# Weight rounding in the first segment of a RetNet and SwiGLU kernel: VectorE's steps regrouped, tiles loaded and rounded later

## The chip, the cores and the metric

One core of one Trainium2 chip runs the kernel. The metric is the device time of one execution in microseconds (us). The kernel before takes 743.69 us, the median of three runs (743.6 to 743.85).

Engines in the profile: PE is TensorE's matmuls, PEld its weight loads, DVE is VectorE, ACT is ScalarE, POOL is GpSimd, SP is SyncE, which issues the loads. "L446" is line 446 of the kernel that was profiled, so one statement has another number in each kernel; each fence says which kernel it shows.

## The reference, cut to what matters

```python
def _attn_ref(q, k, v):               # 4 batches, 8 heads, 768 steps, head size 64
    for t in range(S):
        state = gamma * state + outer(k[t], v[t])
        y[t] = scale * q[t] @ state
def _moe_ref(x, w_gate, w_val, w_out):     # 3072 tokens, 512 -> 1536 -> 512
    g = x @ w_gate
    return (g * sigmoid(g) * (x @ w_val)) @ w_out
```

The three weight matrices reach the kernel as 64-bit floats and have to be rounded to 32-bit ones on the chip.

## The kernel before

The tokens are worked through in segments. Only the first segment matters here. It has three parts: the **retention** of its six chunks (some 40 us), twelve **up blocks** (some 9.5 us each; block f multiplies with up tile f), and the down products. A weight tile that arrives as 64-bit words is rounded in three stages on three engines. The buffer in which it arrives is its raw place, which the next load takes when the last stage is done:

```python
    def convert_a(piece, *own):                  # ScalarE
        if piece in raw:
            d, lo, hi = words_of(piece)
            nc.scalar.activation(d, hi.bitcast(F32), AF.Abs)
            signs[piece] = []
            for i, o in enumerate(own):          # the sign words go to PSUM banks
                nc.scalar.copy(banks[o], hi[:, ts(i, 512)].bitcast(F32))
                signs[piece].append(banks[o])
            nc.scalar.activation(lo.bitcast(F32), lo, AF.Copy, scale=2.0 ** -51, bias=2.0)

    def convert_b(piece):                        # VectorE
        if piece in raw:
            d, lo, hi = words_of(piece)
            nc.vector.tensor_scalar(d, d, ..., op0=ALU.min, op1=ALU.max)           # SBUF only
            u = d.bitcast(U32)
            nc.vector.tensor_scalar(u, u, 3, None, op0=ALU.logical_shift_left)     # SBUF only
            for i, t in enumerate(signs.pop(piece)):
                v = u[:, ts(i, 512)]
                nc.vector.scalar_tensor_tensor(v, t.bitcast(U32), 0x80000000, v,   # reads a bank
                                               op0=ALU.bitwise_and, op1=ALU.bitwise_xor)

    def convert_c(piece):                        # GpSimd, then the next load into the raw place
        if piece in raw:
            d, lo, hi = words_of(piece)
            nc.gpsimd.tensor_tensor(d.bitcast(I32), d.bitcast(I32), lo.bitcast(I32), op=ALU.add)
            del raw[piece]
        load_next(piece[0])
```

An up block works with a scheme of seven products (as Strassen's), each of four TensorE instructions. Wherever products are counted below, one such instruction is meant, so a block has 28. `s1` to `s4` are sums of the block's input, made by VectorE in the retention; the sixteen instructions with T1, T2, B22 and T3 are the products on sums. `sums_t` makes the tile's sums T1, T2 and T4, three subtractions within SBUF. The order of the calls is the order of the instructions on each engine:

```python
    def up(f):
        ...
        product(x, B11, a_up(0, 0));  nc.scalar.copy(p1, x)       # x: bank f % 2
        if f:
            left[f - 1][0]()                       # gates of the block before (product T4, ScalarE)
        if f + 1 < NF:
            sums_t(("up", f + 1, 0))
        product(wb, T1, s1);  nc.scalar.copy(p5, wb)
        for p in at_block[f]:                      # one "down" half tile and up tile f + 2
            convert_b(p)
        for p in at_block[f][::-1]:
            convert_c(p)
        product(x, T2, s2, start=False);  nc.scalar.copy(u2, x)   # accumulates on x, after the copy p1
        product(wb, B22, s4, start=False)
        if f:
            left.pop(f - 1)[1]()                   # gate multiplications of the block before
        tt(hT[:, f, 0], wb, u2, op=add)
        product(x, T3, s3, start=False)
        tt(hT[:, f, 1], x, p5, op=add)
        for i, p in enumerate(at_block[f + 1] if f + 1 < NF else []):
            convert_a(p, *((6, 7) if p[0] == "up" else ((4, 6)[i],)))
        product(z, B21, a_up(0, 1))
        tt(c11, z, p1, op=add)
        left[f] = gates, muls
```

The retention is a list of steps, and the rounding of the first tiles is set between them:

```python
    for n in range(2, len(cs)):
        load_chunk(cs[n], early[4 * n : 4 * n + 4])
        if n in (2, 4):
            load_next("up")
    ...
    retain(7);  convert_a(u0, 0, 1)
    retain(3);  convert_b(u0);  convert_c(u0)
    retain(3);  sums_t(u0)
    retain(3);  convert_a(u1, 2, 3)
    retain(2);  convert_b(u1);  convert_c(u1)
    retain(len(steps))
    convert_a(("down", 0, 0), 4);  convert_a(u2, 6, 7)
```

## Time and profile before

| | before |
|---|---|
| median of three runs | 743.69 us |
| profiled run (742.34 us, not one of the three): span, mean TensorE clock | 740.6 us, 0.998 |
| TensorE busy | 96% of the span |
| one up block (from block 7's to block 8's first product on sums) | 119.69 − 110.03 = 9.66 us |
| 28 products of a block at full rate (the prediction's estimate) | 9.03 us |

On the profile's page, a group of instructions is read like this: line, engine, operation, output and inputs with shapes and count, then busy time and mean ns of one, then the idle time of the engine just ahead of them and who ended most of it. The up products before:

```profile
L435 PE MATMUL bank<-xs,ring 128*128 128x384 f32 x192 | 65.7, 497 | 2.8 <-DVE xs L418 2.8
L435 PE MATMUL bank<-xT,ring 128*128 128x384 f32 x144 | 51.0, 492 | 3.7 <-DVE hT L453 3.7
```

The 3.7 us are the small waits for L453, the last gate multiplication of the block before, one in nearly every block; the 2.8 us are one wait at the end of the retention. There is no long gap anywhere in the up blocks.

### The profile page before, as it was taken

The numbers are of one execution on the slowest core, as the hardware profiler recorded it, in microseconds if no ns is written. First come the engines' busy times: TensorE is split into PE (matmuls) and PEld (weight loads), VectorE is DVE, ScalarE is ACT, GpSimd is POOL, SyncE is SP. The second block draws the span as 40 slices with busy tenths as digits, with TensorE's granted clock in tenths as the row PEclk, the third lists the DMA queues.
The fourth block names the chain that finished last, engine by engine and source line by source line (L and its number), as shares of the span: only waits on it lengthen the run. The fifth ranks groups of instructions, "written<-read, shape, count | busy, mean of one in ns | idle before, by whom it ended". The sixth has DMA issues, their size and how long they took to land.

```text
span 740.6 us, 11633 instructions
## 1 busy us (share of the span) xinstructions
PE 712.9 (96%) x4516; PEld 614.0 (83%) x4516; DVE 482.6 (65%) x829; ACT 241.8 (33%) x484; POOL 244.5 (33%) x152
## 2 busy tenths in 40 slices
PE   5789999999999999999999999999999999999997
PEld 5645555568888999997888999998888899999886
DVE  2899999997595787877454465758426356667420
ACT  2587777421211333321211324332121133233000
POOL 2533333423100547381210173454310053726000
PEclk9999999999999999999999999999999999999999
DMA  9968886458968667670643355660283055540010
GB/s 328 375 214 255 254 265 214 150 205 272 317 220 332 235 228 260 247 270 28 192 180 127 105 209 204 208 205 22 85 308 131 30 200 199 199 150 1 0 58 29
DMA packets 60823, 139.04 MB, mean 188 GB/s; under 512 B 4576, under 2 KB 27616, under 8 KB 60768
## 3 DMA queue, kind: packets, MB, share of 16 engines
q1 hardware_dynamic: 57312, 132.01, 52.2%
q10 hardware_dynamic: 3456, 6.29, 2.4%
q8 instruction: 35, 0.57, 0.3%
q14 instruction: 20, 0.16, 0.1%
HBM read 101.72 MB, written 36.57 MB: 187 GB/s over the span
## 4 chain that ended last, share of the span: by engine, by line
PE 82%; DVE 7%; issue 4%; POOL 2%; DMA 2%; ACT 2%; ACTq 0%; SPq 0%; DVEq 0%; POOLq 0%
PE bank L548 38%; PE bank L632 25%; PE bank L435 6%; PE bank L641 4%; PE bank L328 3%; PE bank L380 3%; PE bank L376 2%; POOL ring L265 2%; DVE ring L277 2%; PE bank L359 1%; DMA hT<-in_q_t_dram 1%; DMA hT<-in_k_t_dram 1%; DMA tab<-in_decays_dram 1%; DVE ring L252 1%; DVE xs L418 0%
## 5 line engine op out<-in xcount | busy, mean ns | idle before, releaser
L548 PE MATMUL bank<-loadp,ring 128*128 128x192 f32 x720 | 140.5, 327 | 2.8 <-ACT midp L513 2.8
L632 PE MATMUL bank<-wot,hsp 128*128 128x256 f32 x576 | 131.5, 383 | 0.0
L548 PEld LDWEIGHTS bank<-loadp,ring 128*128 128x128 f32 x720 | 120.5, 190 | 4.2 <-ACT midp L513 4.0
L632 PEld LDWEIGHTS bank<-wot,hsp 128*128 128x128 f32 x576 | 107.6, 190 | 16.3 <-issue 0.5
L513 DVE TENSOR_TENSOR iop<-bank,iop 128x384 f32<-128x384 f32 x144 | 79.7, 555 | 56.7 <-PE bank L548 53.6
L548 PE MATMUL bank<-xs,ring 128*128 128x192 f32 x432 | 87.8, 326 | 0.0
L513 POOL TENSOR_TENSOR iop<-hsp,midp 128x768 f32<-128x768 f32 x9 | 16.3, 1816 | 189.6 <-ACT hsp L513 149.4
L583 POOL TENSOR_TENSOR hT<-iop 128x768 f32<-128x768 f32 x36 | 66.5, 1848 | 35.8 <-DVE iop L513 35.8
L513 ACT COPY hsp<-bank 128x384 f32<-128x384 f32 x90 | 42.9, 479 | 99.5 <-PE bank L548 88.8
L548 PEld LDWEIGHTS bank<-xs,ring 128*128 128x128 f32 x432 | 73.1, 190 | 0.0
L435 PE MATMUL bank<-xs,ring 128*128 128x384 f32 x192 | 65.7, 497 | 2.8 <-DVE xs L418 2.8
L548 PE MATMUL bank<-xT,ring 128*128 128x192 f32 x324 | 66.2, 327 | 1.1 <-DVE iop L513 1.1
L632 PE MATMUL bank<-wot,hT 128*128 128x256 f32 x288 | 66.3, 383 | 0.0
L435 PEld LDWEIGHTS bank<-xs,ring 128*128 128x128 f32 x192 | 37.2, 194 | 29.5 <-DVE xs L418 3.4
L632 PEld LDWEIGHTS bank<-wot,hT 128*128 128x128 f32 x288 | 53.7, 190 | 8.5 <-issue 1.4
L548 PE MATMUL bank<-hsp,ring 128*128 128x192 f32 x288 | 56.8, 327 | 0.0
L513 DVE TENSOR_TENSOR midp<-bank,midp 128x384 f32<-128x384 f32 x72 | 40.0, 555 | 25.8 <-PE bank L548 24.3
L548 PEld LDWEIGHTS bank<-xT,ring 128*128 128x128 f32 x324 | 54.8, 190 | 2.3 <-DVE iop L513 2.2
L435 PE MATMUL bank<-xT,ring 128*128 128x384 f32 x144 | 51.0, 492 | 3.7 <-DVE hT L453 3.7
L548 PEld LDWEIGHTS bank<-hsp,ring 128*128 128x128 f32 x288 | 48.3, 190 | 0.5 <-ACT hsp L513 0.5
L435 PEld LDWEIGHTS bank<-xT,ring 128*128 128x128 f32 x144 | 26.5, 190 | 25.4 <-issue 9.0
L383 ACT COPY xT<-bank 128x512 f32<-128x512 f32 x24 | 14.1, 587 | 99.4 <-PE bank L380 96.6
(138 smaller groups left out, 983.4 us busy)
## 6 DMA issues: line engine op xcount, KB each, us to landing
ring<-unitt SPq DMA_DIRECT2D x50, 896.0 KB, 4.6
unitt<-ring SPq DMA_DIRECT2D x21, 896.0 KB, 4.6
unitb<-ring SPq DMA_DIRECT2D x12, 896.0 KB, 5.9
ring<-unitb SPq DMA_DIRECT2D x21, 512.0 KB, 5.7
out_dram<-iop ACTq DMA_DIRECT2D x24, 256.0 KB, 4.0
loadp<-in_w_val_dram SPq DMA_DIRECT2D x18, 256.0 KB, 5.8
loadp<-in_w_gate_dram SPq DMA_DIRECT2D x9, 512.0 KB, 6.4
midp<-in_w_out_dram SPq DMA_DIRECT2D x12, 256.0 KB, 3.1
```

The lines of the kernel that those rows point to most:

```text
L265: nc.gpsimd.tensor_tensor(d.bitcast(I32), d.bitcast(I32), lo.bitcast(I32), op=ALU.add)
L277: sub(both, w[:, ds(B22, 2)], w[:, ds(B12, 2)], op=ALU.subtract)
L328: nc.tensor.matmul(sp[i][:, ts(n, P)], kt[r, n], qt[r, n], start=True, stop=True, skip_group_check=True)
L376: nc.tensor.matmul(y[r, ts(n, P)], prev[r, n], qd[r, n], start=(n == 0), stop=False, skip_group_check=True)
L380: nc.tensor.matmul(y[ds(D * i, D), ts(n, P)], vn[:, ts(2 * n + i, D)], a[i][:, n], start=(ci == 0 and n == 0), stop=True, skip_group_check ...
L383: nc.scalar.copy(xT[:, :, c // NCK % 2, ts(ci % L, P)], pairs(y))
L435: nc.tensor.matmul(o, w[:, slot, k], a[:, k], start=(start and k == 0), stop=(stop and k == KH - 1), skip_group_check=True)
L513: events.append((t, len(events), lambda: fn(*args, **kw)))
L548: nc.tensor.matmul(o[:, h], w[:, h, slot], rhs, start=(start and h == 0), stop=True, skip_group_check=True)
L583: by_block(9.5, 13.5, lambda r: pool(to[:, r], u2[:, r], p5[:, r], op=add))
L632: nc.tensor.matmul(o, a[:, k], wot[k][:, slot], start=(start and k == 0), stop=(k == FH - 1), skip_group_check=True)
L641: nc.tensor.matmul(o, a_dn(0, 0, u)[:, k], wot[k][:, B11], start=(k == 0), stop=(k == FH - 1), skip_group_check=True)
```

## The change

What it does: VectorE's SBUF-only steps of both tiles of a block come first and its steps with a bank operand after them, and GpSimd adds the small tile first, so that GpSimd's additions fall beside VectorE instructions with a bank operand. The retention holds less rounding: the first two up tiles are loaded one chunk later, tile 0 is rounded in parts and later, tile 1 after the last sums, tile 2 inside block 0. The down tiles move back by one block up to block 5. ScalarE's table is loaded at the start.

```diff
-    def convert_a(piece, *own):
+    def convert_a(piece, own, part=None):          # the three ScalarE stages can be called apart
...
-    def convert_b(piece):
+    def convert_b(*pieces):
+        for p in pieces:                           # SBUF only: clamp and shift of every piece
...
+        for p in pieces:                           # then the steps with a bank operand
...
-    at_block = [[("down", n // 2, n % 2) for n in range(2 * FH) if f == min(n, NF - 2)] +
-                [("up", f + 2, 0)] * (f + 2 < NF) for f in range(NF)]
+    halves = [("down", n // 2, n % 2) for n in range(2 * FH)]
+    late_piece = {0: ("up", 2, 0), 5: halves[5]}
+    at_block = [[]] + [halves[f - (f < 6) : f + (f > 5) + (f == NF - 2)] +
+                       [("up", f + 2, 0)] * (f + 2 < NF) for f in range(1, NF)]
...
-        if f + 1 < NF:
+        if 1 < f < NF - 1:
             sums_t(("up", f + 1, 0))
+        if f == 0:
+            convert_a(late_piece[f], (6, 7), 0)
         product(wb, T1, s1)
+        convert_b(*at_block[f])
         for p in at_block[f]:
-            convert_b(p)
-        for p in at_block[f][::-1]:
             convert_c(p)
...                                                # parts 1 and 2 of tile 2 follow in block 0
+        elif f in late_piece:
+            convert_a(late_piece[f], (4,))
...
+        if f < 2:
+            sums_t(("up", f + 1, 0))
+        if f in late_piece:
+            convert_b(late_piece[f])
+            convert_c(late_piece[f])
...
+    nc.scalar.activation(warm, warm, AF.Silu)      # table load at the start
...
-        if n in (2, 4):
+        if n in (3, 5):
             load_next("up")
-    for _ in range(4):
+    for _ in range(3):
         load_next("down")
...
-    retain(7);  convert_a(u0, 0, 1)                # (calls joined in one line here)
-    retain(3);  convert_b(u0);  convert_c(u0)
-    retain(3);  sums_t(u0)
-    retain(3);  convert_a(u1, 2, 3)
-    retain(2);  convert_b(u1);  convert_c(u1)
-    retain(len(steps))
-    convert_a(("down", 0, 0), 4);  convert_a(u2, 6, 7)
+    retain(10);  convert_a(u0, (0, 1), 0);  retain(1);  convert_a(u0, (0, 1), 1)
+    retain(1);   convert_a(u0, (0, 1), 2);  retain(2);  convert_b(u0)
+    retain(2);   convert_c(u0)
+    retain(1);   convert_a(u1, (1, 3), 0);  retain(1);  convert_a(u1, (1, 3), 1)
+    sums_t(u0)
+    retain(len(steps))
+    convert_a(u1, (1, 3), 2);  convert_b(u1);  convert_c(u1)
```

## The prediction

> **What bounds the kernel now.** I read the busy shares first: TensorE is busy for 96% of the span. Then I read the stretches of ten microseconds, because the change touches only the first segment. That is the retention (0 to 42 us) and twelve "up" blocks of the weight tiles (42 to 162 us). From 140 us on TensorE is at 10.00 of 10 in nearly every stretch, and no line after that is changed. Columns: PE, PEld, DVE, ACT, POOL busy us (x instructions), TensorE clock, DMA share, GB/s.
>
> ```profile
> 20.00:30.00 10.00, 7.14 (x126) 6.06 (x120) 8.79 (x11) 6.53 (x15) 7.62 (x5) 1.00 1.07 374
> 30.00:40.00 10.00, 7.14 (x100) 5.43 (x100) 9.83 (x16) 4.92 (x15) 4.15 (x4) 1.00 0.84 291
> 40.00:50.00 10.00, 8.63 (x22) 4.94 (x23) 9.10 (x17) 7.98 (x13) 2.49 (x2) 0.83 0.75 234
> 90.00:100.00 10.00, 9.62 (x30) 5.43 (x29) 9.32 (x16) 7.38 (x13) 3.99 (x3) 1.00 0.82 253
> ```
>
> In the retention VectorE is full (9.83) and TensorE waits. In the blocks TensorE has 9.62 of 10 and VectorE 9.3. The timeline shows why: one block, then the end of the retention.
>
> ```profile
> 87.22 2.41 POOL L265 TENSOR_TENSOR ring<-ring,loadp 128x1024 int32<-128x1024 int32 x1 [6.00 <-ACT ring L241]
> 88.08 2.82 PE L435 MATMUL bank<-xT,ring 128*128 128x384 f32 x8 [0.40 <-DVE hT L453]
> 89.59 1.28 POOL L265 TENSOR_TENSOR wot<-wot,midp 128x512 int32<-128x512 int32 x1
> 89.66 1.75 DVE L277 TENSOR_TENSOR ring<-ring 128x512 f32<-128x512 f32 x1 [0.34 <-POOL ring L265]
> 91.45 0.42 DVE L278 TENSOR_TENSOR ring<-ring 128x256 f32<-128x256 f32 x1
> ```
>
> ```profile
> 38.64 2.39 POOL L265 TENSOR_TENSOR ring<-ring,loadp 128x1024 int32<-128x1024 int32 x1 [5.85 <-ACT state L353]
> 38.75 2.56 DVE L418 TENSOR_TENSOR xs<-xT 128x256 f32<-128x256 f32 x1
> 41.35 0.43 DVE L419 TENSOR_TENSOR xs<-xs,xT 128x256 f32<-128x256 f32 x1
> 41.37 7.12 PE L435 MATMUL bank<-xs,ring 128*128 128x384 f32 x16 [2.75 <-DVE xs L418]
> ```
>
> L277 takes 1.75 us beside a GpSimd addition and 0.68 us at 42.49, where GpSimd is idle. L418 takes 2.56 beside L265 and 0.43 alone. Both end about half a microsecond or less after GpSimd does: they wait, they are not slowed. In each block the next tile's first product then waits 0.3 to 0.5 us for L453, the last VectorE gate multiplication. The first sixteen products on xs take 7.12 us; sixteen elsewhere take 5.32. The finer windows give the reason:
>
> ```profile
> 42.00:43.00 1.00, 1.00 (x3) 0.62 (x2) 1.00 (x3) 1.00 (x2) 0.00 (x0) 0.50 0.69 201
> ```
>
> The clock was half from about 41.3 to 44.9, after a gap of 2.75 us.
>
> **What the Trainium skill says.** "SBUF — State Buffer", section "Who interferes with whom": VectorE and GpSimd share one port pair under an exclusive lock. A VectorE instruction with two SBUF inputs, or in a two-port mode, blocks against GpSimd for the whole instruction; with at most one SBUF input outside those modes it doesn't. The trace agrees: L258 (one bank operand) stays at 0.65 us beside GpSimd, L252 goes from 0.69 to 1.04, L255 from 0.69 to 1.65. "TensorE: Matmul & The Clock Gate", Part 1: an idle window of about 3.4 us, free-running, halves the clock until a busy one. Here 2.75 us was enough, and the half clock lasted about 3.6 us. "ScalarE: Activation LUTs", section "What ACT_TABLE_LOAD costs": 1283 ns a load; the trace has 1.28 us, at 0.73 and again at 51.76.
>
> **The change part by part.** I took the new order of every engine and laid the measured durations along it (an estimate by hand).
>
> *Blocks, a gain.* GpSimd now adds the small "down" tile before the "up" tile, and VectorE's four SBUF-only steps precede its three bank steps. So GpSimd's 1.29 + 2.41 us fall beside the bank steps, the gate multiplications and the evictions, all with a bank operand. L277 should fall to 0.68 (1.07 us less) and VectorE from 9.3 to 8.2 us a block. TensorE is then the limit: 28 products at 5.16/16 = 0.3225 us (90.73 to 95.89) make 9.0 us. The last tiles agree: from 136.69 to 145.80, where nothing waits, is 9.1. Before, the eight blocks from 59.06 to 136.69 took 77.6 us; at 9.1 they take 72.8. Worth 4.8 us.
>
> *Loading order.* The first tile (1 MB, 2.8 us at 375 GB/s) now comes after chunk 3, the second after chunk 5. From the bytes moved, chunk 3's queries land at about 15.7 instead of 18.35. Chunk 4 has the same megabytes before it as ever, and lands at about 21.6. So the early arrival is mostly lost again: the fourth scores start at 21.6, and eviction (L383 before, 0.6) and decay (L353, 1.07) put the state addition of chunk 3 at about 26.6.
>
> *Retention, VectorE.* Rounding of tile 0 moves behind that addition: 0.4 + 0.69 + 0.70 + 1.3 us. Then the sums of the second pair 1.75 and the last mask. Uncontended this ends at about 31.4. GpSimd's last scalings (some 1.6 us of blocking) and its addition for tile 0 (2.4 us, which gets the port after the first sum) add 4.0: 35.2. In the old trace the last chunk's eviction starts 2.46 us after its mask (34.24 to 36.70), so 37.6. Then 0.6 + 1.07 + 0.4 + 0.45 and waits of 0.1: the sum s1 is ready at 40.2, against 41.3 now. Worth 1.1 us, perhaps nothing: TensorE idles from about 30.5 to 36, so it may meet that stretch with half clock (up to 0.9 us).
>
> *Tile 1 rounded later, a loss.* This is the term I weigh most. Tile 1 is now rounded after the last sums. After s1 come 1.3 (three sums), 2.7 (rounding), 2.5 (GpSimd's 2.41 and its semaphore): s1 + 6.5. Only then is its raw place free for tile 3. In the trace tile 3's load is issued at 41.06 and its last part lands at 42.0 + 4.9 = 46.9, 5.9 us later. ScalarE rounds tile 3 in 3.4 us **ahead of** the copy of block 1's first product in its program (0.45 us), and TensorE cannot accumulate into that bank before the copy. So the third product group of block 1 can start at s1 + 16.3. TensorE alone would reach it 32 products after s1, at s1 + 10.4. That is a stall of 5.9 us, long enough to halve the clock again (some 1.75 us, as at 41.37). Twelve products (3.9) and four (1.3) later block 2 starts, at s1 + 23.2 = 63.4. Now it starts at 59.06: a loss of 4.3 us, with the earlier s1 already counted.
>
> *Table load.* One load earlier, off the path: 1.28 us of ScalarE at 51.76 saved, worth nothing by itself.
>
> *Sum*: 4.8 gained in the blocks, 4.3 lost ahead of them: 0.5 us net, 743.2. From block 10 on nothing changes.
>
> **Rivals.** (1) The stall at block 1 is small, because the retention ends earlier than I say or the load lands sooner: then the gain is the 4.8, the 1.1 and the half clock's 1.8, together 7.7: 736. For it speaks that the editor plainly meant it; against it, the order of ScalarE and the 5.9 us that the same load took. (2) VectorE stays the limit: the grouped steps still meet GpSimd, because the first blocks' tiles come late and GpSimd's addition slips into the next sums. Then the 4.8 us go to 1 or 2 and the loss stays: 746. Against it, the new block puts GpSimd at 5.2 to 8.9 us and VectorE's SBUF work at 0.7 to 4.5. (3) Transfers: the retention may be set by arrival rather than by VectorE. The 375 GB/s from 10 to 36 us speak for it, but only the order changes, and the last chunk gains just 1 MB: 1 to 2 us either way.
>
> **Range and chances.** The hand schedule says 743.2. Each wait in it is measured, but the retention's end is uncertain by 2 us and the clock by 1.8 us each time. Rival 1 seems likelier than 2, since a grouping like this is made to a purpose; I lean to 742.3, with 738.8 to 745.3 for eight in ten. Two per cent is 14.9 us: faster would need the retention cut by ten and every block stall gone, slower a stall in each block. One chance in a hundred each.
>
> **What would show it.** Right: L277's successor at about 0.7 us from block 3 on, no wait of TensorE for the gate multiplications there, 9.1 us a block; a TensorE gap of 4 to 6 us in block 1, ended by ScalarE's copy, with half clock after it; s1 at 39 to 41 us. Wrong: no gap in block 1 (time near 736), s1 before 37, or blocks still at 9.6 (time near 746). Any difference after 165 us would mean that I missed a dependence on the weight copies written to memory.

## The result

The changed kernel took 745.5 us, the median of six runs (744.03 to 749.11), against 743.61 us (742.61 to 743.85) for the kernel before in the same rounds. The ratio is 1.0031, with a 95% interval of 1.0008 to 1.0055: the same within two per cent, but slower, by about 0.3%. A ratio here is the mean time of one kernel's fast runs over the mean of the other's fast runs of the same rounds, so it is not quite the ratio of the medians that are quoted. The predicted 742.3 us and its range of 738.8 to 745.3 missed: the median lies 0.2 us above the range, on the side where the change loses.

The page of the changed kernel, the groups that answer to those shown of before:

```profile
L446 PE MATMUL bank<-xs,ring 128*128 128x384 f32 x192 | 67.3, 504 | 8.8 <-ACT iop L467 8.8
L446 PE MATMUL bank<-xT,ring 128*128 128x384 f32 x144 | 49.1, 488 | 0.0
```

The waits for the gate multiplications are gone: 3.7 us became 0.0. In their place stand 8.8 us ahead of the products on sums, ended by L467, ScalarE's copy `p1`. The stretches show where they lie (columns as in the prediction):

```profile
30.00:40.00 10.00, 5.19 (x86) 4.31 (x82) 8.77 (x12) 4.70 (x13) 3.71 (x2) 0.99 0.36 134
...
50.00:60.00 10.00, 5.04 (x16) 2.58 (x14) 8.70 (x13) 2.88 (x5) 3.22 (x2) 1.00 0.78 234
90.00:100.00 10.00, 10.00 (x33) 5.90 (x32) 8.75 (x18) 7.64 (x14) 3.69 (x2) 1.00 0.80 254
110.00:120.00 10.00, 8.04 (x25) 4.86 (x26) 8.41 (x18) 8.88 (x15) 3.69 (x2) 1.00 0.79 249
```

In an ordinary stretch of blocks (90 to 100) TensorE went from 9.62 to 10.00 of 10. It stands half idle from 50 to 60, and two microseconds are missing from 110 to 120. At the end of the retention (30 to 40) it is busy for 5.19 us, where it was busy for 7.14 in before.

This profile is of the slowest run, 749.11 us. I ran the changed kernel again and got a typical one (744.9 us), and read from that from here on. It is the first experiment:

**again** (no edit, five rounds): 745.95 us against 743.14, ratio 1.0042 [1.0026, 1.0057].

> The changed kernel, unchanged, for a second profile, since the first one came from the slowest of its six runs (749.1 us; median 745.5). Theory A (late rounding of tile 1 plus half clock): again a TensorE gap of 5.5 to 7 us in block 1 ended by the copy of ScalarE, half clock after it, 9.0 us a block later, a second gap of about 2.2 us near the late down piece; time 744 to 746. Rival B (the loss is an arrival accident of the first profile): no half clock in the retention, the first sum ready near 40, not 44, and the gap in block 1 stays.

The end of block 4 and the start of block 5, from the timelines of the engines, put in order of time (start, duration, engine, line, operation, in brackets the idle time before and its releaser):

```profile
88.66 1.29 POOL L273 TENSOR_TENSOR wot<-wot,ring 128x512 int32<-128x512 int32 x1 [5.34 <-DVE wot L266]
89.94 2.43 POOL L273 TENSOR_TENSOR ring<-ring,loadp 128x1024 int32<-128x1024 int32 x1
93.23 0.68 DVE L285 TENSOR_TENSOR ring<-ring 128x512 f32<-128x512 f32 x1
95.14 5.32 PE L446 MATMUL bank<-xs,ring 128*128 128x384 f32 x16
```

The first subtraction of the sums takes 0.68 us, not 1.75: GpSimd works from 88.66 to 92.37, while VectorE has its bank steps, gate multiplications and evictions. From 68.05 to 77.08 to 86.11 a block takes 9.03 us, the rate that the 28 products allow.

The other side is in block 1:

```profile
44.86 2.42 POOL L273 TENSOR_TENSOR ring<-ring,loadp 128x1024 int32<-128x1024 int32 x1 [10.72 <-DVE ring L266]
...
47.30 0.94 SPq L220 DMA_DIRECT2D loadp<-in_w_val_dram  x2
48.30 0.46 SPq L220 DMA_DIRECT2D loadp<-in_w_gate_dram  x1
...
54.40 1.14 ACT L242 ACTIVATE ring<-loadp 128x1024 f32<-128x1024 f32 x1 [6.13 <-DMA loadp<-in_w_gate_dram]
...
57.58 0.46 ACT L467 COPY iop<-bank 128x384 f32<-128x384 f32 x1
```

GpSimd's addition of tile 1 ends at 47.28, and only then is tile 3's load issued, at 47.30. ScalarE waits for it 6.13 us and starts at 54.40. The copy `p1` of block 1 stands behind it in ScalarE's program and comes at 57.58. TensorE alone, in the same run:

```profile
41.94 5.33 PE L446 MATMUL bank<-xs,ring 128*128 128x384 f32 x16
...
58.09 6.25 PE L446 MATMUL bank<-xs,ring 128*128 128x384 f32 x12 [5.67 <-ACT iop L467]
...
107.79 4.14 PE L446 MATMUL bank<-xs,ring 128*128 128x384 f32 x12 [2.17 <-ACT iop L467]
```

A wait of 5.67 us, then twelve products in 6.25 us where 4.14 would do (the clock was 0.50 from 56 to 60). And a second wait of 2.17 us in block 6, which I had not predicted. Its reason, on the timeline of all engines:

```profile
100.97 0.69 DVE L259 TENSOR_SCALAR wot<-wot 128x512 f32<-128x512 f32 x1
...
102.23 0.69 DVE L266 SCALAR_TENSOR_TENSOR wot<-bank,wot 128x512 uint32<-128x512 uint32 x1
...
102.96 0.64 ACT L246 COPY bank<-ring 128x512 f32<-128x512 f32 x1 [2.21 <-DVE wot L266]
```

At block 5 the change rounds two down pieces: the "late" one and the one for block 6. Both have their sign words in bank 4. ScalarE's copy for the second (L246) waits 2.21 us until VectorE has read the first (L266), and block 6's `p1` stands behind it.

So my first theory: the regrouping gains about 5 us, and tile 1's late rounding (with bank 4) loses more. The rivals were that the loading order or the rest of the retention's new order loses, and that the regrouping gains little.

### The profile page after: what moved, and what is told of

It reads as the page before. It is cut to its first block, busy times and chain, and to the rows that moved or that the text cites. A ratio compares the mean times of both kernels' runs of the same rounds, so it can differ in the third digit from the quotient of the medians.

```text
span 747.3 us, 11647 instructions
## 1 busy us (share of the span) xinstructions
PE 714.9 (96%) x4516; PEld 618.2 (83%) x4516; DVE 471.7 (63%) x829; ACT 239.1 (32%) x484; POOL 243.5 (33%) x153
## 4 chain that ended last, share of the span: by engine, by line
PE 89%; DMA 3%; DVE 3%; ACT 2%; issue 1%; SPq 0%; POOL 0%; ACTq 0%; DVEq 0%; POOLq 0%
PE bank L571 38%; PE bank L655 25%; PE bank L446 13%; PE bank L664 4%; PE bank L391 3%; PE bank L339 3%; PE bank L387 2%; PE bank L370 1%; DMA hT<-in_q_t_dram 1%; DMA hT<-in_k_n_dram 1%; DMA loadp<-in_w_gate_dram 1%; DMA hT<-in_k_t_dram 1%; DVE xs L430 0%; POOL ring L273 0%; ACT bank L246 0%
## 5 line engine op out<-in xcount | busy, mean ns | idle before, releaser
L655 PEld LDWEIGHTS bank<-wot,hsp 128*128 128x128 f32 x576 | 107.7, 190 | 16.3 <-issue 0.5
L536 POOL TENSOR_TENSOR iop<-hsp,midp 128x768 f32<-128x768 f32 x9 | 16.3, 1814 | 189.9 <-ACT hsp L536 149.8
L446 PE MATMUL bank<-xs,ring 128*128 128x384 f32 x192 | 67.3, 504 | 8.8 <-ACT iop L467 8.8
L446 PE MATMUL bank<-xT,ring 128*128 128x384 f32 x144 | 49.1, 488 | 0.0
```

Of the source, the lines that this page charges most:

```text
L446: nc.tensor.matmul(o, w[:, slot, k], a[:, k], start=(start and k == 0), stop=(stop and k == KH - 1), skip_group_check=True)
L536: events.append((t, len(events), lambda: fn(*args, **kw)))
L655: nc.tensor.matmul(o, a[:, k], wot[k][:, slot], start=(start and k == 0), stop=(k == FH - 1), skip_group_check=True)
```

## The experiments

Each kernel was built from before or after by the edit shown, gave a correct result, and was timed against the kernel before in the same rounds. All ratios are to the kernel before.

| run | edit | us (median) | ratio [95%] |
|---|---|---|---|
| again | changed kernel | 745.95 | 1.0042 [1.0026, 1.0057] |
| blocks_alone | before + regrouping only | 737.06 | 0.9919 [0.9906, 0.9931] |
| order_alone | blocks_alone + loading order | 736.2 | 0.9908 [0.9891, 0.9924] |
| group_only | before + VectorE's grouping only | 739.33 | 0.9948 [0.9934, 0.9963] |
| gp_order_only | before + GpSimd's order only | 743.32 | 1.0005 [0.9988, 1.0022] |
| u1_late | blocks_alone + tile 1 late | 741.79 | 0.9981 [0.9966, 0.9996] |
| bank6 | changed, late down piece in bank 6 | 744.24 | 1.0011 [0.9999, 1.0023] |
| late3 | changed, tile 3 later | 743.69 | 0.9998 [0.9982, 1.0014] |
| fill1 | changed, TensorE kept busy in block 1 | 744.6 | 1.0017 [0.9991, 1.0044] |
| u1_early | changed, tile 1 back | 745.36 | 1.0034 [0.9993, 1.0075] |
| u1_early6 | u1_early + bank 6 | 741.56 | 0.9979 [0.996, 0.9999] |
| u01_early6 | u1_early6, tile 0 back too | 738.48 | 0.9933 [0.992, 0.9945] |
| all_late | own version | 749.68 | 1.0089 [1.0074, 1.0104] |
| late_split | own version | 741.7 | 0.998 [0.9965, 0.9994] |
| late_split_order | own version | 739.27 | 0.9943 [0.9929, 0.9958] |
| tail_fix | own version | 736.42 | 0.9904 [0.9887, 0.992] |
| tail_fix2 | own version | 738.42 | 0.9929 [0.9906, 0.9951] |

The kernel before stood at 743.12 to 743.25 us in all these rounds.

### The regrouping by itself

**blocks_alone**: the kernel before with nothing but the new order inside a block.

```diff
-    def convert_b(piece):
+    def convert_b(*pieces):          # SBUF steps of all pieces, then the bank steps
...
-        for p in at_block[f]:
-            convert_b(p)
-        for p in at_block[f][::-1]:
+        convert_b(*at_block[f])
+        for p in at_block[f]:
             convert_c(p)
```

> The kernel before, with only the grouping of the block conversions (SBUF steps of both tiles first, down tile first on GpSimd); retention, loads and the early rounding of tiles 1 and 2 as before. Theory A: blocks of 9.0 to 9.1 us and no stall in block 1, so about 4.5 us less than before: 738.5 to 739.5. Rival B (the blocks' gain is given back somewhere later, for instance to the writes of weight copies): 742 to 744.

Measured: 737.06 us, 6.1 below before. Its TensorE, from the end of the retention:

```profile
42.12 1.80 PE L440 MATMUL bank<-xs,ring 128*128 128x384 f32 x4 [2.76 <-DVE xs L423]
...
62.33 5.32 PE L440 MATMUL bank<-xs,ring 128*128 128x384 f32 x16
...
71.36 5.32 PE L440 MATMUL bank<-xs,ring 128*128 128x384 f32 x16
```

The retention ends as before, and every block then takes 9.03 us (62.33 to 71.36). Rival 2 of the prediction has fallen, and the gain was there to be had.

**order_alone**: blocks_alone with the loading order of the change (`n in (3, 5)`, three down pieces ahead).

> The grouped blocks with the old retention, but the loads in the changed order (tile 0 after chunk 3, tile 1 after chunk 5, three down pieces). Theory A: within 1.5 us of 737.1 either way, since the bytes ahead of chunk 4 are the same and the rounding order is the old one. Rival B: 2 us or more slower, because tile 0 arrives 3 to 4 us later and everything in VectorE's program stands behind its rounding.

Measured: 736.2 us. The loading order loses nothing; the 0.9 us below blocks_alone were measured in other rounds and on another chip, and the intervals overlap.

**group_only and gp_order_only** take the regrouping apart: the first keeps GpSimd's old order (up tile first) under VectorE's new one, the second is the kernel before with the other loop alone.

```diff
-        for p in at_block[f][::-1]:      # gp_order_only: this line and nothing else
+        for p in at_block[f]:
             convert_c(p)
```

> The grouped VectorE order of the blocks with GpSimd's old order (up tile first). Theory: the down addition still meets the next tile's first subtraction, which stays at 1.76 us; nothing else is moved off the path, so 742 to 744. Rival: the grouping alone is all of it: 736.5 to 737.5.

> The kernel before with one change: GpSimd adds the down tile first, the up tile second; VectorE's order is the old one. Theory (exclusive port): the first subtraction of the next tile falls from 1.76 to 0.68 us, but now the down addition of 1.29 us meets the up tile's clamp, which then takes up to 1.5 us instead of 0.69; so VectorE keeps about 9.2 us a block, and the gain is a part of the 6 us of the grouped version: 738 to 742. Rival: GpSimd's order alone is all of it: 736.5 to 737.5.

Both expectations failed. In group_only VectorE still meets GpSimd (timeline of group_only):

```profile
98.10 1.29 POOL L270 TENSOR_TENSOR wot<-wot,midp 128x512 int32<-128x512 int32 x1
98.17 1.77 DVE L282 TENSOR_TENSOR ring<-ring 128x512 f32<-128x512 f32 x1 [0.34 <-POOL ring L270]
```

The subtraction still takes 1.77 us, yet the kernel gained 3.8 us: a block takes 9.28 us (89.97 to 99.25), because VectorE comes to the gate multiplications earlier in the block (5.46 us after the first product on sums, 89.97 to 95.43; in before 5.86, 81.06 to 86.92). In gp_order_only the subtraction is down to 0.69 us and nothing is gained, because the contact has only moved (timeline of gp_order_only):

```profile
94.78 1.60 POOL L265 TENSOR_TENSOR wot<-wot,midp 128x512 int32<-128x512 int32 x1 [3.38 <-DMA loadp<-in_w_gate_dram]
95.27 1.67 DVE L255 TENSOR_SCALAR ring<-ring 128x1024 uint32<-128x1024 uint32 x1
```

GpSimd's small addition now starts amid VectorE's clamp of the up tile, and the shift after the clamp takes 1.67 us in place of 0.69. The two edits are worth 3.8 and −0.2 us alone, and 6.1 together.

### Tile 1, bank 4 and the half clock

**u1_late** adds only tile 1's late rounding to blocks_alone (half of its sign words go to bank 1 in place of 2, as in the change).

```diff
-    convert_a(u1, 2, 3)
-    retain(2)
+    convert_a(u1, 1, 3)
+    retain(len(steps))
     convert_b(u1)
     convert_c(u1)
-    retain(len(steps))
```

> The grouped blocks with the old retention (737.1 us), but tile 1 rounded after the last sums, as in the change; nothing else moved. Theory A (late rounding of tile 1 delays tile 3's load, and ScalarE's rounding of tile 3 stands ahead of the copy of block 1's first product): the first sum is ready some 2 us sooner, at about 40, since GpSimd's addition no longer meets it; then a TensorE gap of 4 to 6 us in block 1 ended by ScalarE's copy and half clock after it; 740 to 742. Rival B (the order of the loads makes the loss): about 735 to 737 and no gap in block 1.

741.79 us, 4.7 above blocks_alone: as the theory had it, in time. The shape was another, though: four waits of 2.86, 1.79, 1.21 and 1.04 us, 6.9 together, no half clock after them, and s1 ready at 40.58. So that the time came out as expected is partly luck.

**late3** moves tile 3's rounding behind the copy that it blocked, and its sums to the end of block 2.

```diff
-    late_piece = {0: ("up", 2, 0), 5: halves[5]}
+    late_piece = {0: ("up", 2, 0), 1: ("up", 3, 0), 5: halves[5]}
...
-                       [("up", f + 2, 0)] * (f + 2 < NF) for f in range(1, NF)]
+                       [("up", f + 2, 0)] * (1 < f < NF - 2) for f in range(1, NF)]
...
-            convert_a(late_piece[f], (4,))
+            convert_a(late_piece[f], (6, 7) if f == 1 else (4,))
```

> The changed kernel with tile 3 rounded in the middle of block 1 (ScalarE's part after the copies of block 1's first products), its sums at the end of block 2. Theory A: the gap of block 1 before the third product group is gone and its half clock with it; 6 to 8 us less than the changed kernel in the same rounds: 737 to 740. Rival B (the retention's late end is the loss): at most 2 us less.

743.69 us: 2.3 us better (by ratios 3.3), not 6 to 8. In block 1 the wait is gone; it stands in block 2, where tile 4's rounding is now ahead of the copy (TensorE of late3):

```profile
65.07 7.13 PE L446 MATMUL bank<-xs,ring 128*128 128x384 f32 x12 [3.05 <-ACT iop L467]
```

The chain of tiles is late as a whole; taking one tile out of the way shows the next.

**bank6** is one number in the changed kernel.

```diff
-            convert_a(late_piece[f], (4,))
+            convert_a(late_piece[f], (6,))
```

> The changed kernel with the sign words of the late down piece in bank 6 instead of bank 4, one number changed. Theory: the gap of 2.2 us in block 6 comes from ScalarE's waiting for VectorE to free bank 4 before the next down piece; without it 2.0 to 2.4 us less than the changed kernel. Rival: the gap comes from VectorE's extra 1.5 us in block 5; then it stays.

744.24 us, 1.7 less by the medians and 2.3 by the ratios. The sixteen products of block 6 run without a long break (TensorE of bank6), where in **again** they had a wait of 2.17:

```profile
105.73 5.65 PE L446 MATMUL bank<-xs,ring 128*128 128x384 f32 x16
```

The second, unpredicted wait was the shared bank.

**fill1** computes block 1's T1 product five times, to keep TensorE from idling (the product overwrites its bank, so the result stays right).

```diff
-        product(wb, T1, s1)
+        for _ in range(5 if f == 1 else 1):
+            product(wb, T1, s1)
```

> The changed kernel with the second product group of block 1 computed five times over into the same bank (same values), so that TensorE is busy in most of the gap of block 1. The gap's length is set by ScalarE and should stay. Theory: the half clock after the gap goes, so the next twelve products take 3.9 to 4.2 us instead of 6.1 to 6.9, and the time falls by about 2 us: 743 to 744. Rival: the clock is not a matter of the idle gap; nothing falls, or 5 us are added.

```profile
51.89 6.61 PE L446 MATMUL bank<-xs,ring 128*128 128x384 f32 x20
59.29 4.14 PE L446 MATMUL bank<-xs,ring 128*128 128x384 f32 x12 [0.79 <-ACT iop L467]
```

With TensorE busy, the twelve products take 4.14 us, not 6.25. So the 2.1 us are the clock and not the products. In the time it is 1.35 us by the medians, and the interval reaches 1.0044, so the size is not settled by the time.

### What is left: undoing the change's retention tile by tile

The theory so far would have tile 1's place as the main loss in the changed kernel. **u1_early** undoes just that.

```diff
     sums_t(u0)
-    retain(len(steps))
     convert_a(u1, (1, 3), 2)
     convert_b(u1)
     convert_c(u1)
+    retain(len(steps))
```

> The changed kernel with tile 1's last rounding steps (ScalarE's scaling of the low words, VectorE's four steps, GpSimd's addition) placed back before the rest of the retention, everything else as changed. Theory (the late rounding of tile 1 delays GpSimd's chain of tiles 1, 2 and 3 and so the third product group of block 1): that group no longer waits for the first weights' loads, the gap of 5.67 us of block 1 falls under 1.5 us, s1 of the last chunk comes later by 1 to 3 us because GpSimd's addition and the VectorE steps meet the last sums, and the sum is 740 to 742 us, 4 to 6 below the changed kernel; the gap of 2.2 us in block 6 stays. Rival (the rest of the retention's new order is what costs: the parts of tile 0's rounding, the table load, the later scores): the time stays at 744 to 746 us and the gap of block 1 stays over 4 us.

745.36 us, 0.6 below **again**, with runs from 742.03 to 748.91: **the theory failed here**. TensorE of u1_early:

```profile
35.67 2.35 PE L391 MATMUL bank<-iop,hsp 128*64 128x128 f32 x15 [4.53 <-DVE iop L345]
...
43.64 7.12 PE L446 MATMUL bank<-xs,ring 128*128 128x384 f32 x16 [1.94 <-DVE xs L429]
```

and the reason on VectorE and GpSimd of the same run, a fence for each engine:

```profile
41.03 2.55 DVE L429 TENSOR_TENSOR xs<-xT 128x256 f32<-128x256 f32 x1
```

```profile
40.92 2.38 POOL L273 TENSOR_TENSOR ring<-ring,loadp 128x1024 int32<-128x1024 int32 x1 [6.99 <-DVE ring L266]
```

The wait of block 1 did fall from 5.67 to 1.73 us, with no half clock there. But tile 1's addition now meets the first of the retention's last four sums: L429 takes 2.55 us in place of 0.42, the first product on sums starts at 43.64 in place of 41.94, and the first sixteen take 7.12 us at half clock in place of 5.33. What the block gains here, the retention takes. How much is left over, these six runs don't settle.

**u1_early6** adds bank 6.

> As u1_early and the sign words of the late down piece in bank 6 instead of 4. If the two losses (tile 1's place and bank 4) are all that the changed kernel has beyond the grouping of the blocks and the loading order, it comes to 736 to 739 us, 1.7 to 2.3 us below u1_early, and no gap over 1 us is left between blocks 2 and 10. If it stays over 741 us, a third cause in the retention is still missing.

741.56 us: a third cause is missing. It is still 5.4 us above order_alone, which has the same grouping and the same loading order. But tile 1's place is not worth nothing: bank6 differs from u1_early6 by it alone, and took 744.24 us, 2.7 more (2.4 by the ratios; other rounds, another chip, before at 743.14 and 743.15); in the profiles block 3's first product on sums starts at 78.64 and 75.98. TensorE of u1_early6:

```profile
37.68 2.35 PE L391 MATMUL bank<-iop,hsp 128*64 128x128 f32 x15 [4.39 <-DVE iop L345]
...
45.66 5.43 PE L446 MATMUL bank<-xs,ring 128*128 128x384 f32 x16 [3.07 <-DVE xs L429]
```

TensorE waits 4.39 us for L345, the last chunk's mask on VectorE. Ahead of it in VectorE's program now stand tile 0's rounding and sums.

**u01_early6** puts tile 0's rounding back as well; tile 2 stays in block 0.

```diff
-    retain(10);  convert_a(u0, (0, 1), 0);  ...  convert_a(u1, (1, 3), 2);  convert_b(u1);  convert_c(u1)
+    retain(7);   convert_a(u0, (0, 1))
+    retain(3);   convert_b(u0);  convert_c(u0)
+    retain(3);   sums_t(u0)
+    retain(3);   convert_a(u1, (1, 3))
+    retain(2);   convert_b(u1);  convert_c(u1)
     retain(len(steps))
```

> The changed kernel with tiles 0 and 1 rounded where the kernel before rounds them, bank 6 for the late down piece, tile 2 still in block 0, table load and loading order as changed. If tile 0's later place is the third cause: the wait of 4.4 us for the last chunk's masks is gone, the first product on the sums starts at 41.5 to 42.5 us in place of 45.66, and the time is 737 to 739 us, 3 to 4 under u1_early6; what is left over 736.2 us is tile 2's place, 1 to 2 us in blocks 1 and 2. If tile 0's place is not it, the time stays at 740 to 742 us.

738.48 us, 3.1 below u1_early6, as expected for tile 0. TensorE of u01_early6:

```profile
33.75 1.09 PE L387 MATMUL bank<-hsp,state 64*64 64x128 f32 x16 [1.12 <-ACT xT L394]
...
41.19 7.12 PE L446 MATMUL bank<-xs,ring 128*128 128x384 f32 x16 [2.75 <-DVE xs L429]
...
55.20 4.14 PE L446 MATMUL bank<-xs,ring 128*128 128x384 f32 x12 [1.74 <-ACT iop L467]
```

The 4.4 us for the mask are gone, and the first product on sums starts at 41.19. What remains is the wait of 1.74 us in block 1 and 0.71 us in block 2. The first comes from tile 2, which the change rounds inside block 0 (ScalarE of u01_early6):

```profile
52.51 1.23 ACT L246 COPY bank<-loadp 128x512 f32<-128x512 f32 x2 [2.52 <-DVE ring L266]
```

ScalarE's copy of tile 3's sign words to banks 6 and 7 waits 2.52 us until VectorE has read tile 2's there (L266), and block 1's `p1` stands behind it: the pattern of bank 4 again. No run gave tile 2 other banks, so what this wait alone costs is not shown. In all, 2.3 us are left to order_alone.

The landmarks of TensorE in the profiled runs (starts of the first product on sums; one run each):

| | block 0 | block 3 | block 11 | span |
|---|---|---|---|---|
| before | 41.37 | 71.31 | 148.38 | 740.6 |
| order_alone | 41.84 | 71.17 | 143.41 | 734.9 |
| again (changed) | 41.94 | 77.08 | 151.75 | 743.1 |
| u1_early | 43.64 | 75.64 | 150.35 | 741.7 |
| u1_early6 | 45.66 | 75.98 | 148.58 | 740.0 |
| u01_early6 | 41.19 | 73.19 | 145.73 | 737.1 |

From block 3 to block 11 the changed kernel takes 74.67 us, order_alone 72.24 and before 77.07: of the 2.4 us between the first two, bank 4 is 2.1 (bank6 takes 72.60 us there, from 78.64 to 151.24). All the rest is lost ahead of block 3.

### Own versions

I tried to round late in every block from the start. **all_late** puts all rounding behind T2's copy in a block; **late_split** lets the SBUF steps come ahead of the last eviction and the bank steps behind it, and splits tile 1 in the same way around the retention's last sums; **late_split_order** adds the loading order; **tail_fix** and **tail_fix2** spread the sums of the down tiles at the end.

```diff
+    late = [[halves[f]] + [("up", f + 2, 0)] * (f + 2 < NF) for f in range(NF)]
+    late[NF - 2], late[NF - 1] = halves[NF - 2 :], []
...                                            # late_split, in up(f), against before
         nc.scalar.copy(u2, x)
+        for i, p in enumerate(late[f]):
+            convert_a(p, (6, 7) if p[0] == "up" else ((4, 6)[i],))
...
         tt(hT[:, f, 1], x, p5, op=add)
+        if f + 1 < NF:
+            sums_t(("up", f + 1, 0))
+        convert_b(*late[f], part=0)            # SBUF steps (all_late: both parts here)
         product(z, B21, a_up(0, 1))
         tt(c11, z, p1, op=add)
+        convert_b(*late[f], part=1)            # bank steps
+        for p in late[f]:
+            convert_c(p)
...                                            # tail_fix against late_split_order
-    for j in (1, 2, 3):
-        sums_t(("down", j, 0))                 # now one each inside up(NF - 1)
...                                            # tail_fix2: tiles 1 and 2 there, and behind the last gates:
+    sum_h(1, 0)
+    for j in (3, 4, 5):
+        sums_t(("down", j, 0))
```

> A version meant to be faster than both: old load order, tile 0 as before, tile 1's SBUF steps before the last sums and its bank steps after them, and in every block both tiles' rounding after the block's own sums of the next tile, with ScalarE's part after the copies of that block. Expected: first product on the sums at about 40 without half clock, no gap in blocks 1 and 2, blocks of 9.0 us: 732 to 735. If ScalarE's or GpSimd's part comes too late for the next tile, gaps of 1 to 3 us appear in some blocks: 736 to 742.

> The failed version with both tiles' rounding late in each block, mended: in it ScalarE's gate waited for the eviction that stood behind VectorE's bank steps, 10.3 us a block. Now the eviction stands between the SBUF steps and the bank steps. Expected: 9.0 us a block, first product on the sums at about 40 without half clock, no gap in blocks 1 and 2: 731 to 735. If GpSimd's additions now end too late for the next tile's sums, 736 to 742.

> The same with the loads in the changed order. The order alone was worth between 0 and 2 us; expected within 1.5 us of the other version, and not slower than 735.

> My late_split_order (739.27 us) with the sums of down tiles 1, 2 and 3 moved into the last up block, one each behind the multiplications, the second output and the last eviction, in place of three in a row before it. Theory (the three sums stand on VectorE beside GpSimd's sums of down tile 0 and ahead of the gate multiplications of block 10, and the first down product waits for those 4.94 us): the gap falls under 2 us, the half clock behind it goes, and the time is 731 to 735 us. Rival (the down products then wait for the later sums as long): 738 to 740 us.

> tail_fix with the sums of down tiles 3, 4 and 5 behind the gate multiplications of the last block, the last eviction ahead of tile 2's sums, and the first sum of the hidden rows ahead of tile 3's. Theory (only the order on VectorE holds the multiplications back, 152.04 us in tail_fix where the gates end at 149.1): the multiplications end by 150.5 us, the wait of 3.29 us falls under 1 us and with it the half clock, and the time is 731.5 to 734 us. Rival: the later sums of tiles 3 to 5 make the T products wait as long, 735 to 737 us.

all_late was a miss, 749.68 us: a block takes 10.34 us, as ScalarE's gate waits for an eviction that stands behind VectorE's bank steps (ScalarE of all_late):

```profile
62.37 0.49 ACT L458 ACTIVATE bank<-iop 128x384 f32<-128x384 f32 x1 [2.15 <-DVE iop L495]
```

late_split mended that (9.03 us a block). late_split_order has the first product on sums at 39.21 and block 11's at 138.64, 4.8 us ahead of order_alone, and lost it all (739.27 us, where not over 735 was expected) in a wait of 4.94 us and the half clock after it, where VectorE makes the down tiles' sums beside GpSimd. tail_fix shortened that wait but not enough (736.42 us; a wait of 3.29, then twelve products in 4.54 us). tail_fix2 removed it, missed its expectation all the same (738.42 us), and waits a step later, in the next segment's scores:

```profile
161.34 2.67 PE L336 MATMUL bank<-loadp 64*128 64x128 f32 x16 [2.52 <-DVE midp L342]
```

The best kernels are order_alone (736.2 us) and tail_fix (736.42), which can't be told apart; both beat the two given kernels.

## Why the prediction was wrong

**Right: the mechanism of the gain.** L277's successor at 0.68 us, no wait for the gate multiplications, 9.03 us a block against the predicted 9.1. Predicted 4.8 us; alone it measured 6.1 by the medians, 4.9 by the spans of the profiled runs (740.6 to 735.7), and 4.8 from block 3 to block 11 (77.07 to 72.24). Two readings in its working were wrong and did no harm. VectorE's 9.3 us are of a stretch of 10 us and not of a block; the change took them to 8.75. And no L258 runs beside GpSimd in the trace of before; **again** shows what was claimed of it, two instructions of L266 in 1.28 us from 97.47, beside GpSimd's addition at 97.69.

**Right: the mechanism of the loss at block 1.** The gap, its releaser (ScalarE's copy behind tile 3's load) and the half clock after it all came. s1 was ready at 40.83 us in **again**, predicted 40.2.

**The step that failed is the one headed "Tile 1 rounded later, a loss", in its size.** It put block 2's start at "s1 + 23.2 = 63.4", a loss of 4.3 us. In **again** it was 65.47 (four products of 0.32 us after the group that starts at 64.18): 6.4 us later than 59.06. The 2.1 us split as follows: s1 itself 0.6 (the last mask began at 35.15 as predicted, though its sum of 31.4 and 4.0 is 35.4 and not 35.2, but the eviction came 3.34 us after it and not 2.46); the third product group at s1 + 17.26 and not s1 + 16.3, 1.0, since the load took 7.1 us from issue to ScalarE's start (47.30 to 54.40) and not 5.9; and 7.38 us and not 6.9 from there to block 2, 0.5, which is the half clock, mostly (6.25 us for twelve products where the working had 3.9 + 1.75).

**A term was missing: bank 4.** The sum went from block 2 to block 10 without a wait. Block 6 had one, 2.17 us in the profile, and bank6 measured 1.7 to 2.3 us for undoing it. The diff shows both uses of bank 4 at block 5; I did not follow banks through the late piece.

Together: predicted −0.5 us at block 10; in **again** block 10 starts at 140.14 (138.85 and four products), before at 136.69: +3.45. 2.1 and 2.4 us of loss came on top, and the blocks without block 6 gave 0.6 more (72.24 us for eight blocks in place of 72.8). Block 11 and after took 0.9 us less than in the profile of before, which I did not follow.

**The lean was wrong.** The hand schedule said 743.2; I leaned to 742.3 "since a grouping like this is made to a purpose". That is no measurement. The range was too narrow at its upper end: the text itself named an uncertainty of 2 us for the retention and 1.8 us for each half clock.

**The name of the step was only half right.** The loss is in all three tiles. Tile 1's place alone, undone, gave back 0.6 us by the medians in u1_early, whose runs spread by 6.9 us, and 2.7 us with bank 6 in both kernels (bank6 to u1_early6); neither is the whole. Going by medians down from **again** to order_alone, in the order in which they were undone: tile 1's place 0.6, bank 4 3.8, tile 0's place 3.1, tile 2's place (with the table load and the down tiles' shift, which u01_early6 still has) 2.3; together 9.75 us, against 6.9 us gained by regrouping and loading order (743.14 to 736.2). The first two of these are no prices: by the spans in the table of landmarks they are 1.4 and 1.7 us, and bank 4 measured 1.7 to 2.3 us when it was undone first, so u1_early's spread may account for the difference. Tile 1 late costs 4.7 us on blocks_alone. So only the sum is shown, not a fixed price for each. The prediction counted the retention's new order as a gain of 1.1 us, "perhaps nothing". In **again** s1 is ready 0.5 us sooner than in before (40.83, 41.31). With tile 1 early, tile 0's later place was a loss of 3.1 us (u1_early6 to u01_early6); what it costs with tile 1 late, no run shows.

**The half clock was named, but left out of the sum.** The working allowed "up to 0.9 us" for it in the retention and did not add it to s1. In **again** the clock was 0.50 from 36 to 40, and the eviction came 0.9 us later after its mask than in before (3.34 and 2.46 us), more than the 0.6 us by which s1 was late. After the gap it was counted as 1.75 us; twelve products took 2.1 us more.

**Open.** No run takes the table load away by itself; only its 1.28 us at 51.76 is gone from ScalarE, and nothing is known of its worth. The changed kernel's twelve runs spread from 744.03 to 749.11 us, those of before in the same rounds from 742.18 to 743.95. In the slowest, the stretch from 20 to 30 us has clock 0.66, and s1 was ready at 44.4. In u1_early the three runs over 747 us have mean clocks of 0.986 to 0.989, the other three 0.993 to 0.997. That the spread comes from when the fourth chunk's queries land and where TensorE's clock then stands is argued from this, not tested.

## What to carry to other kernels

Work that is "moved out of the way" of one stage is not gone: follow each moved tile through all its engines, its bank and its raw place to the load that the place sets free, because the next tile's chain starts there. Where VectorE and GpSimd hold each other up, put VectorE's SBUF-only steps together and GpSimd's work beside the steps with a bank operand, and change both orders: here VectorE's alone gave 3.8 of 6.1 us, and GpSimd's alone only moved the contact (−0.2). And test a named cause by undoing it in the changed kernel as well as by adding it to the old one: here adding tile 1's late rounding cost 4.7 us, and undoing it gave 0.6 in one kernel and 2.7 in another.

## What the Trainium skill lacked or had wrong

- "TensorE: Matmul & The Clock Gate", Part 1, gives one idle window of about 3.4 us, free-running, as what halves the clock, and its summary advises against gaps over about 3 us. Here shorter gaps were enough, though not always. After 2.75 us in before and in u01_early6 the sixteen products took 7.12 us, and after 2.76 us in blocks_alone the clock was 0.50 from 44 to 46. After 2.86 us in u1_late and 3.07 us in u1_early6 it stayed at 1.00. So the advice as a number doesn't hold, and these runs don't show what decides.
- "SBUF — State Buffer", section "Who interferes with whom", says that the first to issue holds the shared pair and the other fully blocks. This case agrees, and adds who comes next: GpSimd's addition, begun during one VectorE instruction, got in before the next. In u1_early L429 took 0.42 us from 31.27 and L430, right after it, 2.51 us, while the addition ran from 31.48 to 33.93. No sentence there says that the pair is given away between back-to-back instructions.
- No page that I read gives the time from a load's issue to its data when other loads are in the queue: for a 1 MB tile 7.1 us in **again** (47.30 to 54.40, when ScalarE starts on it), against 5.9 us to landing in the trace of before. Why the two differ was not looked into.
